# The last bit step of a weight conversion: low word rounded into the high word on ScalarE, high word masked in place on VectorE

## The chip, the core and the metric

One core of a Trainium2 chip runs the whole kernel. The metric is the device time of one execution in microseconds; 447.03 us is the median of three runs before the change. The engines are named as the profile names them: PE is TensorE (matmuls; PEld its weight loads), DVE is VectorE, ACT is ScalarE, POOL is GpSimd, SP is the engine that issues most DMAs.

## The reference

An mLSTM cell feeds a two-layer MLP with a quick gelu. Cut to what matters:

```python
# cell: B, H, S, D = 4, 8, 768, 40, step by step over t
C = f_stab * C + i_stab * outer(v_t, k_t);  n = f_stab * n + i_stab * k_t
y[t] = sigmoid(o_t) * (C @ q_t) / max(|n . q_t|, 1)
# bridge: (B, H, S, D) -> x of (3072, 320)
# MLP
'w_in':  np.random.randn(320, 2048).astype(np.float32) * (1.0 / np.sqrt(320))
'w_out': np.random.randn(2048, 320).astype(np.float32) * (1.0 / np.sqrt(2048))
h = x @ w_in
g = h * (1.0 / (1.0 + np.exp(-1.702 * h)))
out = g @ w_out
```

The factor behind `astype` is a 64-bit float, so both weight matrices arrive as 64-bit floats. The change concerns only how they become 32-bit floats.

## The kernel before

The sequence is cut into six windows of 128 steps. For each window the kernel does the cell as attention within the window plus a carried state, then the MLP for the window's 512 rows: up-projection, gelu, down-projection. The first window uses plain 32-bit matmuls (`up`, L657 and L666; `down`, L835). Later windows use other forms (L806, L888, L963) with weights that are split further on the core. The order on every engine is written out by hand: the program text is the order.

**The conversion.** The weights come in 20 pieces of 128 x 512 numbers, each fetched (L177, on SP's queue) as pairs of 32-bit words into a tile `bits`; `lo` is every even word and `hi` every odd one. Pieces 0, 1, 3, 4, 5, 6, 8 and 9 make w_in, pieces 2 and 7 make w_in_x (its last 64 rows), pieces 10 to 19 make w_out. The high word of a 64-bit float holds the sign, 11 bits of exponent and 20 of mantissa; a 32-bit float wants 8 bits of exponent and 23 of mantissa. Each piece passes through these steps:

- `convert_high` (L253, ScalarE): absolute value of the high word, read as a 32-bit float, into the destination.
- `convert_low` (L257, ScalarE): the low word times 2^-29, rounded to an integer from 0 to 8, in place. These are the three missing mantissa bits.
- `convert_clamp` (L269, VectorE): limits on the destination, so that the exponent fits.
- `convert_sign` (L274 and L276, VectorE): the destination is shifted left by 3 and its two top bits are cleared; then the two top bits of the high word (sign and top exponent bit) are put in with a two-operand operation.
- `convert_add` (L282, VectorE): the rounded low word is added as an integer. This add appears in the profile as a custom operation on 1024 16-bit elements.

The call order is: piece 0 among the attention of the first window, with high, clamp and sign before the low step; piece 1 in the seam behind it (high, then low, then the VectorE steps); pieces 1 to 5 finish in and after the seam into `up(0, 0)`; pieces 6 to 16 stand around the later pairs of up-projections; piece 17 stands before the first block of the down-projection (L1163 to L1168), pieces 18 and 19 before its fifth and sixth blocks. In between, VectorE does the gates, the transposes (L415) and the products with the weights (L493) for the attention of window 1, whose matmuls (L490, L534, L542) are laid between the blocks of the down-projection (L835).

On ScalarE the gelus (L672), copies (L409, L574) and exps (L452, L463) share the queue with the two conversion steps. GpSimd masks the attention weights (L454, L470) and scales values (L619).

Of the kernel before, what the change touches and what calls it, by code (L numbers as in the profile page):

```python
# [8 lines left out]
FP = mybir.dt.float32  # L9
FR = mybir.dt.float32r  # L10
U32 = mybir.dt.uint32
BF = mybir.dt.bfloat16
AF = mybir.ActivationFunctionType
OP = mybir.AluOpType
# [17 lines left out]
def kernel(  # L32
# [37 lines left out]
    op = ctx.enter_context(tc.tile_pool(name="op", bufs=2))  # L70
# [5 lines left out]
    V, A, G, T = nc.vector, nc.scalar, nc.gpsimd, nc.tensor  # L76
# [58 lines left out]

    w_in_bits, w_out_bits = moe_w_in.bitcast(U32), moe_w_out.bitcast(U32)
    rest_bits = w_in_bits[256:DM, :].rearrange("k (j two m) -> two k j m", two=2, m=256)
# [27 lines left out]
    bits = {}  # L165

    def fetch(n):
        if n < 3 or 10 <= n < 13:
            bits[n] = win.tile([128, 512, 2], U32, tag="wb", name="bits")
        elif n == 17:  # L170
            bits[n] = t_flat[:, at_bits:at_bits + 1024].bitcast(U32).rearrange("p (a two) -> p a two", two=2)
        else:
            bits[n] = (gp if 6 <= n < 10 else sp).tile([128, 512, 2], U32, tag="g", name="bits")
        for r, c, src in pieces[n][1]:
# [17 lines left out]

    small = t_flat[:, at_const:].bitcast(BF)
    idle, ident_b, neg_mask = (small[:, n * 128:n * 128 + 128] for n in range(3))
# [26 lines left out]
    for j in range(3):  # L221
        V.tensor_scalar(out=pick[j * BH:(j + 1) * BH, :], in0=ident[0:BH, 0:BH], scalar1=-1.0, scalar2=None,
                        op0=OP.mult)
# [16 lines left out]
    def words(n):  # L240
        return bits[n][:, :, 0], bits[n][:, :, 1], pieces[n][0]
# [5 lines left out]
    def convert_begin(n):  # L247
        convert_high(n)
        convert_low(n)
# [4 lines left out]

    def convert_low(n):
        lo, hi, dst = words(n)
        A.activation(out=lo, in_=lo, func=AF.Copy, scale=2.0 ** -29)  # L257

    def convert_end(n):
        convert_mid(n)  # L260
        convert_add(n)

    def convert_mid(n):
        convert_clamp(n)
        convert_sign(n)
# [5 lines left out]
    def convert_sign(n):  # L271
        lo, hi, dst = words(n)
        dst_u = dst.bitcast(U32)
        V.tensor_scalar(out=dst_u, in0=dst_u, scalar1=3, scalar2=0x3FFFFFFF, op0=OP.logical_shift_left,  # L274
                        op1=OP.bitwise_and)
        V.scalar_tensor_tensor(out=dst_u, in0=hi, scalar=0xC0000000, in1=dst_u, op0=OP.bitwise_and,  # L276
                               op1=OP.bitwise_or)

    def convert_add(n):
        lo, hi, dst = words(n)  # L280
        dst_u = dst.bitcast(U32)
        V.tensor_tensor(out=dst_u, in0=dst_u, in1=lo, op=OP.add)  # L282


    def split(engine, dst, x, left, part):

        first, second, third = (dst[j * BH:(j + 1) * BH, :] for j in range(3))
        engine.tensor_copy(out=first, in_=x)
        engine.tensor_tensor(out=left, in0=x, in1=first, op=OP.subtract)
        engine.tensor_copy(out=part, in_=left)  # L290
        A.copy(out=second, in_=part)
        engine.tensor_tensor(out=left, in0=left, in1=part, op=OP.subtract)
        engine.tensor_copy(out=third, in_=left)
# [5 lines left out]
    def gates(w):  # L299
# [8 lines left out]
        if w == 0:  # L308
            room = work.tile([L, H, D1], FP, tag="u", name="room").rearrange("p h d -> p (h d)")
            neg, part = room[0:BH, 0:L], room.bitcast(BF)[0:BH, 2 * L:3 * L]  # L310
            V.tensor_tensor(out=neg, in0=f_run, in1=i_sb[w], op=OP.subtract)
            split(G, a3, neg, neg, part)
        V.tensor_tensor_scan(out=m_run, data0=ones, data1=a, initial=m, op0=OP.mult, op1=OP.max)
        if w == 0:

            room = work.tile([L, H, D1], FP, tag="u", name="room").rearrange("p h d -> p (h d)")
            left, part = room[0:BH, 0:L], room.bitcast(BF)[0:BH, 2 * L:3 * L]
            split(V, m3, m_run, left, part)
# [669 lines left out]
    for b in range(B):  # L988
        if b >= 2:
            transposes(0, b)  # L990
            open_first(b - 2)
            weights(0, b)
            values(0, b - 2)
            scale(0, 0, b - 2, 2)
        else:
            weights(0, b)
        if b == 0:
            convert_high(0)
            transposes(0, 1)
        scores(0, b)  # L1000
        if b == 0:
            convert_mid(0)
        if b == 1:
            columns(0)
            convert_low(0)
            convert_add(0)
# [8 lines left out]
    seam(0, 0, 1)  # L1015
    seam(0, 1, 0)
    convert_low(1)

    def last_seam():
        seam(0, 1, 1)  # L1020
        convert_mid(1)
        convert_add(1)
        for p in (2, *converted[0][0]):
            convert(p)
# [217 lines left out]
```

## Time and profile before

| what | us |
|---|---|
| median of three runs (445.67 to 449.79) | 447.03 |
| the profiled execution | 443.5 |
| its span | 441.8 |
| TensorE busy, 4967 matmuls | 435.5 |
| VectorE busy, 701 instructions | 350.6 |
| ScalarE busy, 536 instructions | 245.6 |
| GpSimd busy, 133 instructions | 129.9 |

The prices of the conversion, from groups by line and shape (mean of one, ns): L253 681 to 684, L257 687, L269 418 to 525, L274 427 to 618, L276 692 to 731, L282 691 to 789, all on 128 x 512 numbers. The larger means contain instructions that ran beside GpSimd's work; the medians are 683, 687, 420, 427, 692 and 693.

How to read it: the span is the profiled stretch on the core, and the execution's own time is 1.7 us longer. In timelines the columns are start, duration, engine, line, operation, output and input tiles, shapes and count; what stands in brackets is idle time before and what ended it. In the chain of waits the columns are start, duration and what ran. A line number is that of the kernel before.

### The profile page before, as it was taken

What the parts mean: (1) busy time and instruction counts of PE and PEld (TensorE: products, weight loads), DVE (VectorE), ACT (ScalarE), POOL (GpSimd) and SP (SyncE); (2) the same over time, 40 slices, a digit from 0 to 9 for tenths busy, and PEclk for the clock granted to TensorE, in tenths of its full rate; (3) what the DMA queues carried; (4) which work ended last, traced back from release to release, by engine and by line L of the source; (5) the groups of instructions that cost most, each with busy time, mean ns of one, the idle gap of its engine ahead of it and who ended that gap; (6) DMA issues with size and microseconds to landing.
All of it is one profiled execution on the core that took longest, in us unless ns stands there. A gap on an engine that the chain in (4) does not pass through costs nothing.

```text
span 441.8 us, 12222 instructions
## 1 busy us (share of the span) xinstructions
PE 435.5 (99%) x4967; PEld 380.3 (86%) x4967; DVE 350.6 (79%) x701; ACT 245.6 (56%) x536; POOL 129.9 (29%) x133
## 2 busy tenths in 40 slices
PE   8999999999999999999999999999999999999996
PEld 6867887777889999888999888999888999888996
DVE  6888999989998877778686779686769666988990
ACT  5686779802987601677701586900486902397720
POOL 6401328530076600145600034700035610022100
PEclk9999999999999999999999999999999999999999
DMA  8999999228679238979026978306998306710000
GB/s 169 174 301 223 247 252 188 61 60 204 154 206 185 38 77 237 239 117 173 6 63 184 282 94 177 45 27 155 306 136 158 62 19 146 255 75 0 6 27 30
DMA packets 130008, 61.37 MB, mean 139 GB/s; under 512 B 102128, under 2 KB 122592, under 8 KB 129952
## 3 DMA queue, kind: packets, MB, share of 16 engines
q1 hardware_dynamic: 120512, 54.86, 56.6%
q10 hardware_dynamic: 8768, 4.28, 3.4%
q0 software_dynamic: 672, 1.46, 1.2%
q8 instruction: 39, 0.64, 0.6%
q14 instruction: 17, 0.14, 0.2%
HBM read 49.76 MB, written 10.81 MB: 137 GB/s over the span
## 4 chain that ended last, share of the span: by engine, by line
PE 79%; DMA 7%; DVE 6%; SPq 4%; ACT 2%; issue 1%; DVEq 0%
PE p_out L888 28%; PE p L806 17%; PE p_h L806 17%; PE p L963 6%; PE p_out L835 4%; SPq L132 3%; DMA bits<-in_moe_w_out_dram 3%; PE p L534 2%; PE p L542 2%; DMA q_sq<-in_q_dram 2%; PE p L490 2%; DMA bits<-in_moe_w_in_dram 1%; PE p L633 1%; DMA v_st<-in_v_dram 1%; DVE qT L415 1%
## 5 line engine op out<-in xcount | busy, mean ns | idle before, releaser
L856 POOL TENSOR_TENSOR g<-g 128x512 f32<-128x512 f32 x16 | 20.6, 1294 | 119.5 <-ACT g L784 119.5
L888 PE MATMUL p_out<-w_out,g 128*128 128x160 f32 x384 | 55.2, 300 | 0.0
L888 PEld LDWEIGHTS p_out<-w_out,g 128*128 128x128 f32 x384 | 53.1, 190 | 0.5
L765 ACT ACTIVATE x_high<-xT 128x512 fp32r<-128x512 f32 x10 | 6.3, 630 | 76.4 <-DVE xT L603 76.4
L784 ACT ACTIVATE g<-g 128x512 f32<-128x512 f32 x80 | 46.4, 628 | 2.6 <-DVE g L825 2.3
L823 ACT ACTIVATE g<-p 128x512 f32<-128x512 f32 x40 | 21.7, 596 | 36.4 <-PE p L806 35.0
L825 DVE SCALAR_TENSOR_TENSOR g<-p,g 128x512 f32<-128x512 f32 x40 | 25.7, 682 | 18.4 <-ACT g L823 10.1
L463 ACT ACTIVATE wt<-wt,cols 128x64 f32<-128x64 f32 x160 | 38.9, 335 | 0.1
L893 DVE TENSOR_TENSOR o_sb<-o_sb,p_out 128x160 f32<-128x160 f32 x56 | 16.7, 316 | 26.9 <-PE p_out L888 26.8
L888 PE MATMUL p_out<-t_sb,s 128*128 128x160 f32 x256 | 37.8, 301 | 0.0
L888 PEld LDWEIGHTS p_out<-t_sb,s 128*128 128x128 f32 x256 | 35.5, 190 | 0.2
L835 PE MATMUL p_out<-w_out,g 128*128 128x320 f32 x128 | 35.7, 436 | 0.0
L835 PEld LDWEIGHTS p_out<-w_out,g 128*128 128x128 f32 x128 | 23.9, 190 | 9.6
L825 DVE SCALAR_TENSOR_TENSOR g<-p_h,g 128x512 f32<-128x512 f32 x40 | 26.1, 683 | 5.8 <-PE p_h L806 5.0
L657 PE MATMUL p_h<-xT,w_in 128*128 128x256 f32 x128 | 29.8, 385 | 0.7 <-ACT xT L574 0.7
L657 PEld LDWEIGHTS p_h<-xT,w_in 128*128 128x128 f32 x128 | 23.6, 190 | 6.1 <-issue 2.2
L823 ACT ACTIVATE g<-p_h 128x512 f32<-128x512 f32 x40 | 23.3, 595 | 8.5 <-PE p_h L806 8.5
L470 POOL TENSOR_SCALAR_AFFINE_SELECT wt<-wt 64x1024 f32<-64x1024 f32 x20 | 24.6, 1231 | 6.9 <-ACT wt L463 5.8
L806 PE MATMUL p_h<-x_diff,w_diff 128*128 128x512 f32 x80 | 25.1, 394 | 0.0
L806 PE MATMUL p_h<-x_rest,w_rest 128*128 128x512 f32 x80 | 25.0, 394 | 0.0
L806 PE MATMUL p<-x_rest,w_rest 128*128 128x512 f32 x80 | 25.0, 394 | 0.0
L806 PE MATMUL p<-x_diff,w_diff 128*128 128x512 f32 x80 | 25.0, 393 | 0.0
(226 smaller groups left out, 1045.9 us busy)
## 6 DMA issues: line engine op xcount, KB each, us to landing
w_diff<-w_row SPq DMA_DIRECT2D x16, 512.0 KB, 5.8
wt<-m_row SPq DMA_DIRECT2D x20, 256.0 KB, 5.4
bits<-in_moe_w_in_dram SPq DMA_DIRECT2D x8, 512.0 KB, 7.6
out_dram<-o_sb SPq DMA_DIRECT2D x24, 160.0 KB, 3.1
q_sq<-in_q_dram SPq DMA_DIRECT2D x10, 320.0 KB, 9.1
eo<-in_o_gate_dram SPq DMA_DIRECT2D x5, 640.0 KB, 5.5
bits<-in_moe_w_out_dram SPq DMA_DIRECT2D x8, 320.0 KB, 5.8
q_sq<-x_row SPq DMA_DIRECT2D x10, 256.0 KB, 2.7
```

The costliest lines, as they stand in the source:

```text
L463: A.activation(out=x[:, h, :], in_=x[:, h, :], func=AF.Exp, scale=-1.0, bias=cols[w][:, c * PH + h:c * PH + h + 1])
L470: G.affine_select(out=r, in_=r, compare_op=OP.is_ge, fill=0.0, base=0, pattern=[[0, PH], [1, HL]], channel_multiplier=-1)
L657: T.matmul(ph[j][i][:, t], w_in[f // 4][:, c, f % 4 * 128:f % 4 * 128 + 128], x[:, c, t], start=(first and c == 0 and n == 0), stop=(not f ...
L784: A.activation(out=g, in_=g, func=AF.Gelu_apprx_sigmoid)
L806: T.matmul(dst[i], a(i), x, start=(first and m == which[0]), stop=(last and m == which[-1]))
L823: A.activation(out=g[:, i, :], in_=side[i], func=AF.Copy, scale=-BASE)
L825: V.scalar_tensor_tensor(out=g[:, i, :], in0=main[i], scalar=1.0 + 1.0 / BASE, in1=g[:, i, :], op0=OP.mult, op1=OP.add)
L835: T.matmul(po, gs[w, f // 2][:, f % 2, b * L:(b + 1) * L], w_out_sb[f // NH][:, f % NH, :], start=(f == 0), stop=(f == NF - 1))
L856: G.tensor_tensor(out=a10, in0=a00, in1=a10, op=OP.subtract)
L888: T.matmul(po, a(f), b[:, f, :], start=(f == 0), stop=(f == NH - 1))
L893: V.tensor_tensor(out=dst, in0=x, in1=po, op=OP.add)
L963: T.matmul(dst, g_part[n, b, f // 2][:, f % 2], wo[n, f][0][:, wo[n, f][1]], start=(f == order[0] and n < 2), stop=(f == order[-1] and n > 0))
```

## The change

The low step on ScalarE writes its rounded integer as 16 bits into the lower half of the high word, in place of the whole low word. VectorE, in place of the two-operand operation on the high word and the destination, masks the high word in place, keeping its two top bits and its four lowest. The add then brings in the masked high word: sign, top exponent bit and rounded low bits in one.

```diff
+U16 = mybir.dt.uint16
...
     def convert_low(n):
         lo, hi, dst = words(n)
-        A.activation(out=lo, in_=lo, func=AF.Copy, scale=2.0 ** -29)
+        half = bits[n].rearrange("p a two -> p (a two)").bitcast(U16).rearrange("p (a four) -> p a four", four=4)
+        A.activation(out=half[:, :, 2], in_=lo, func=AF.Copy, scale=2.0 ** -29)
...
         V.tensor_scalar(out=dst_u, in0=dst_u, scalar1=3, scalar2=0x3FFFFFFF, op0=OP.logical_shift_left,
                         op1=OP.bitwise_and)
-        V.scalar_tensor_tensor(out=dst_u, in0=hi, scalar=0xC0000000, in1=dst_u, op0=OP.bitwise_and,
-                               op1=OP.bitwise_or)
+        V.tensor_scalar(out=hi, in0=hi, scalar1=0xC000000F, scalar2=None, op0=OP.bitwise_and)
...
     def convert_add(n):
         lo, hi, dst = words(n)
         dst_u = dst.bitcast(U32)
-        V.tensor_tensor(out=dst_u, in0=dst_u, in1=lo, op=OP.add)
+        V.tensor_tensor(out=dst_u, in0=dst_u, in1=hi, op=OP.add)
```

The number of instructions and their order on every engine stay as they are. The waits differ: the low step waits for ScalarE's own high step (for piece 0, for VectorE's mask); the mask waits for the DMA and ScalarE's low step, and no longer for the shift; the add waits for VectorE alone (for piece 0, for ScalarE's low step).

## The prediction

> **What bounds the kernel now.** I read the page's slices first, then the timelines of TensorE and VectorE over the stretch in which weights are converted (8 to 88 us), then the chain of waits there, then single lines for prices. The slices show TensorE busy throughout at the full granted clock.
>
> ```profile
> PE   8999999999999999999999999999999999999996
> DVE  6888999989998877778686779686769666988990
> PEclk9999999999999999999999999999999999999999
> ```
>
> A busy TensorE is not yet a bound, since waiting matmuls can count as busy. So I looked at its pace in the timeline (columns: start, duration, line, tile, shapes, count):
>
> ```profile
> 23.91 1.13 PE L657 MATMUL p_h<-xT,w_in 128*128 128x256 f32 x4 [0.70 <-ACT xT L574]
> ...
> 34.22 3.72 PE L657 MATMUL p_h<-xT,w_in 128*128 128x256 f32 x16
> 37.87 1.99 PE L666 MATMUL p_h<-xT,w_in_x 64*128 64x512 f32 x8
> 39.79 3.72 PE L657 MATMUL p_h<-xT,w_in 128*128 128x256 f32 x16
> ...
> 82.91 4.57 PE L835 MATMUL p_out<-w_out,g 128*128 128x320 f32 x16
> 87.54 1.32 PE L534 MATMUL p<-v_st,wt 64*64 64x41 f32 x63
> ```
>
> The first row starts with the last wait that this view names for TensorE: 0.70 us at 23.91. Afterwards every group starts where the former ends and sixteen L657 rows take 3.72 us wherever they stand; a group held up by data would be longer than its twins. TensorE has 63.95 busy us in the 64 us from 24 to 88. From 107 us on the chain of waits is matmul after matmul to the end. So from 23.9 us on the time is TensorE's own work, and the converting engines matter only where they are late.
>
> How late they are now, VectorE's timeline, one piece and the junction at 86 us:
>
> ```profile
> 51.56 0.42 DVE L269 TENSOR_SCALAR w_out<-w_out 128x512 f32<-128x512 f32 x1
> 52.01 0.43 DVE L274 TENSOR_SCALAR w_out<-w_out 128x512 uint32<-128x512 uint32 x1
> 52.47 0.69 DVE L276 SCALAR_TENSOR_TENSOR w_out<-bits,w_out 128x512 uint32<-128x512 uint32 x1
> 53.30 0.69 DVE L282 CUSTOM_DVE_ANT_0 w_out<-bits,w_out 128x1024 uint16<-128x1024 uint16 x1
> 53.91 0.42 DVE L269 TENSOR_SCALAR w_out<-w_out 128x512 f32<-128x512 f32 x1
> ...
> 86.27 2.35 DVE L493 TENSOR_TENSOR wt<-p,wt 128x1024 f32<-128x1024 f32 x2
> ```
>
> A piece costs 53.91 - 51.56 = 2.35 us: starts 0.45, 0.46, 0.83 and 0.61 us apart. TensorE's deadlines, from the starts of the matmuls that read a piece: the first w_in_x piece is done at 29.44, read at 29.63 (0.2 us spare); piece 4 at 34.15, read in the second half of the group at 34.22, about 36.1 (1.9); piece 14 at 63.41, read in the second w_out block, after 66.3 (2.9). The junction: L493's first half ends at 86.27 + 1.23 = 87.50, and L534, which reads it, starts at 87.54; but TensorE's own L835 group before it ends at 82.91 + 4.57 = 87.48. VectorE and TensorE arrive there together. The chain of waits walks back through VectorE at this point:
>
> ```profile
> 84.83 0.70 DVE w_out L276
> ...
> 86.27 1.23 DVE wt L493
> 87.50 0.04 issue
> 87.54 1.32 PE p L534 x63
> ```
>
> This is the trap of the case: the chain names L276, the very operation that goes, yet without it TensorE would be ready only 0.06 us sooner.
>
> **Part 1, L276 becomes a one-operand mask (20 times).** The trace has no in-place operation on every second word, so bounds from rows: the nearest by kind is L274, a one-operand bit operation on 512 uint32 words, 427 ns; the other end is L276 itself, 692 ns, if the stride loses the faster rate; farther out is L415's transpose of 512 elements, 1,091 ns, the row in which VectorE writes with a stride (every fourth word). I take 427 ns: the stride costs nothing in the rows that have it, since L276 reads every second word in 692 ns, as the contiguous L775 does (692 ns, same kind and size). The add behind it waited for ScalarE and VectorE (0.83 us between starts for 0.69 us of work); now it waits for VectorE alone, which may save up to 0.83 - 0.69 - 0.03 = 0.11 us more (0.03 is the gap between clamp and shift, which has one wait). A piece gains 0.27 to 0.37 us, 20 pieces 5.3 to 7.4 us of VectorE. A mask of 692 ns gains 0 to 0.11 us, one of 1,091 ns loses 0.29 to 0.40 us per piece.
>
> What comes of it at the end: at the first w_in_x piece nothing, as L666 follows its predecessor directly; at the junction 0.06 us. What is late next there is TensorE itself. Cover: TensorE's back-to-back groups; without it the end would move by what the junction shows, below.
>
> [...]
>
> **Part 2, the low word (ScalarE, L257, 20 times).** Output becomes 16 bits wide at every eighth byte. L253 (strided read, dense write) takes 683 ns and L257 (strided both ways) 687 ns, so stride is free there; narrow writes appear only small and dense (L291, 32x128 bf16, 294 ns). Taken: 687 ns; bounds 0.6 us (a copy of that size, L672's 0.60) to twice 687 if narrow writes cost double. The new output overlaps what the high step reads, so the low step now waits for the high step before it on the same engine. Starts are 0.57 us apart now; a dependent start comes at 0.68 + 0.04 (L742 starts 0.04 us after L741 ends), so 0.15 us more per piece. Queued behind it on ScalarE are the gelus: three pieces stand before the first one (31.14), which moves by 0.45 us, and the groups at 59.87 to 63.30 by the same. The banks of the first gelu are needed at 34.22 and it ends at 32.23, 2 us spare; ScalarE then idles 3.11, 2.00 and 2.57 us ahead of later gelus and catches up. Cost at the end: 0. If narrow writes doubled, three pieces would cost 2.1 us plus 0.45 against those 2 us, so at most 0.6 us. Mask behind low: the mask starts 0.9 us after the high step ended, the low step ends 0.72 us after it, so it is on time.
>
> **Part 3, piece 0 turns round.** There the mask is issued before the low step, so ScalarE's low step (11.49) must wait for VectorE's mask, which starts at 11.58 and ends between 12.0 and 12.6 (L276 took 1.00 us there, beside GpSimd's L454). ScalarE stands 0.6 to 1.2 us; behind it queue both L409 copies, the tanh and the exps of batch 2. TensorE's L479 at 14.11 needs the copies, done at 13.35: 0.76 us spare, so it slips 0 to 0.5 us. At 16.32 ScalarE waited 1.63 us for L406 anyway, and at 22.82 it waited 0.99 us for the DMA of piece 1, behind which stands the L574 copy that TensorE awaits at 23.91. That DMA was issued at 17.11 behind queue SP's earlier ones, untouched by the change. Cost: 0, at most 0.3 us.
>
> DMAs: fetches that reuse a bits buffer still wait for the same add; some also for ScalarE, long done. No instruction changes place on any queue.
>
> **Sum.** -0.06 + 0 + 0 = about -0.1 us on the profiled execution: 443.5 us (span 441.8 and 1.7 around it) becomes 443.4. That execution lies 3.5 us under the median of the three runs; I carry the difference to the median: 447.03 - 0.1 = 446.9 us.
>
> **Rivals.**
> - *The conversions were the bound after all.* For it: the chain through L276 between 66 and 87 us, VectorE busy 58.13 of 64 us. Against: TensorE's even pace. If only the stretch behind the last idle counted (pieces 18 and 19 and part of 17), 1.1 us: 445.9; if all 7.4 us came out, 439.6. Chance 0.06, of which 0.04 beyond 1%.
> - *Slower: the strided write in place is slow.* Mask at L415's price, 0.29 to 0.40 us more per piece. VectorE last idled at 40.71 (0.74 us); after that pieces 8 to 19 run behind each other into L493, which has no spare. 12 x 0.29 to 0.40 = 3.5 to 4.8 us: 450.5 to 451.8. It decides as soon as the mask with its waits exceeds today's 0.83 us, and passes 1% at 4.5/12 = 0.37 us more, a mask of about 1.06 us. For it: L415. Against: L276's and L257's free strides. Chance 0.12, half of it beyond 1%.
> - *ScalarE's new waits reach TensorE* (parts 2 and 3): 0.3 + 0.6 us, 447.8. Against: idle times of 1 to 3 us behind each. Chance 0.04.
> - *The mask gains nothing* (692 ns): time as forecast, and inside its 0.78.
>
> **Numbers.** The forecast has 0.78. One percent is 4.5 us, about the 4.1 us spread of the three runs and what a measurement can tell from no change. Faster by more: 0.04 from the first rival and 0.01 of scatter, 0.05. Slower: 0.06 from the second and 0.03 of scatter and the unseen, 0.09. Same: 0.86. The forecast's own scatter is some 2.4 us either way (the runs lie 1.4 below to 2.8 above their median); the range goes to 444.5, and up to 449.8 towards the slower rival.
>
> **What would show it.** Right: masks of some 0.43 us; pieces some 2.0 us apart; VectorE with new idle time before L493; L534 still straight behind L835 near 87.5; L657 groups still 3.72 us. ScalarE's low step starting some 0.72 us behind the high one. Wrong: a mask over 0.8 us, a gap in TensorE before the L534 or L666 groups, or a first L657 moved from 23.9.

## The result, and the profile after

The change made the kernel slower by about half a percent. Over 21 runs of each kernel, taken beside each other, the median is 448.3 us after (446.27 to 451.83) against 445.7 us before (443.87 to 449.79); the ratio is 1.0054, with a 95% interval of 1.0033 to 1.0074, which is 1.5 to 3.3 us. The profiled execution of after took 448.44 us, with a span of 446.7; that of before had 443.5 and 441.8.

In the changed kernel almost every line number is one higher: L259 is the low step, L278 the mask, L283 the add, L464 the exps, L119 the copies into q_sq, L491 the score matmuls, L836 the down-projection. The slices and busy times of its page:

```profile
PE 438.5 (98%) x4967; PEld 382.2 (86%) x4967; DVE 342.2 (77%) x701; ACT 258.6 (58%) x536; POOL 129.4 (29%) x133
...
PE   8999999899999999999999999999999999999996
...
DVE  5886974969989777779686779686778656978990
...
PEclk9999999899999999999999999999999999999999
```

VectorE has lost 8.4 us of work (350.6 before), as the change means it to. ScalarE has gained 13 us (245.6 before). And TensorE's row and its clock's row both have an 8 in the eighth slice, 78 to 89 us, where they had a 9. The reason for ScalarE's 13 us stands in its costliest new group (operation, shapes and count, then busy us, mean ns of one, idle time before):

```profile
L259 ACT ACTIVATE bits<-bits 128x512 uint16<-128x512 uint32 x19 | 25.8, 1359 | 1.4 <-DVE bits L278 0.9
```

The low step takes 1,359 ns instead of 687. TensorE's timeline over the stretch shown of before:

```profile
25.20 1.13 PE L658 MATMUL p_h<-xT,w_in 128*128 128x256 f32 x4 [0.52 <-ACT xT L575]
...
65.46 8.78 PE L836 MATMUL p_out<-w_out,g 128*128 128x320 f32 x32
...
84.04 1.16 PE L491 MATMUL p<-qT,kT 40*64 40x64 f32 x64 [1.72 <-DVE state L643]
85.52 1.48 PE L491 MATMUL p<-qT,kT 40*64 40x64 f32 x64 [0.32 <-DVE state L643]
86.92 5.88 PE L836 MATMUL p_out<-w_out,g 128*128 128x320 f32 x16
92.73 1.14 PE L535 MATMUL p<-v_st,wt 64*64 64x41 f32 x64
```

Before, the score matmuls of both halves were one group:

```profile
80.89 2.10 PE L490 MATMUL p<-qT,kT 40*64 40x64 f32 x128
```

L535 starts 5.19 us later than L534 did before (87.54); some groups on, the first L807 matmul is 4.90 us later (111.88 against 106.98), and the difference in span is 4.9. These rows add up to it within 0.1 us:

- 1.29 us lie before 25.20, where the first row stood at 23.91. The whole up-projection keeps that shift and adds nothing: the first L836 group starts at 65.46 against 64.10.
- 1.72 + 0.32 = 2.04 us are a gap before the two halves of L491, which waits for VectorE's state. Before, L490 had no wait.
- 0.32 + 1.31 us are matmuls at a lower clock: the second half of L491 takes 1.48 instead of 1.16, the sixteen L836 rows 5.88 instead of 4.57. The granted clock is 0.89 from 80 to 88 us and 0.90 from 88 to 96.

Shorter stretches show that these two means hide a step (bounds, length, busy us and count of TensorE, its weight loads, VectorE, ScalarE and GpSimd, granted clock, DMA share, GB/s):

```profile
85.00:86.00 1.00, 0.69 (x48) 0.55 (x41) 0.97 (x3) 1.00 (x2) 0.30 (x1) 1.00 0.14 45
...
87.00:88.00 1.00, 1.00 (x2) 0.76 (x3) 0.97 (x3) 1.00 (x2) 0.00 (x0) 0.50 0.99 264
...
90.00:91.00 1.00, 1.00 (x5) 0.71 (x4) 1.00 (x2) 0.97 (x2) 1.00 (x1) 1.00 0.00 0
```

Read in stretches of 0.1 us, the clock is 0.50 for 3.41 us, from 86.2 to 89.6, and 1.00 on both sides. Half of 3.41 us is 1.7 us of matmul time, and the two rows lost 1.63.

The sum is 4.96. The first part isn't the change: the start of this row jumps between profiles, 23.79 and 23.93 in two kernels below that contain most of the change, 25.91 in one that keeps the old conversion, and up to 26.10 in others. Without it the profile shows 3.7 us lost, more than the 2.6 of the medians; the lower clock, as the runs below show, doesn't come in every execution.

Where the gap comes from, the chain of waits tells (start, duration, what ran):

```profile
72.70 1.54 ACT wt L464 x7
...
76.60 0.62 ACT q_sq L119
...
78.85 3.02 DVE qT L416 x3
...
84.96 0.51 DVE state L643
85.52 1.48 PE p L491 x64
```

Sixteen exps and two copies on ScalarE, then VectorE's transposes, then the state, then TensorE. Before, ScalarE had these rows:

```profile
58.90 1.08 ACT L672 ACTIVATE g<-p_h 128x512 f32<-128x512 f32 x2 [2.57 <-PE p_h L666]
...
68.50 3.93 ACT L463 ACTIVATE wt<-wt,cols 128x64 f32<-128x64 f32 x16
72.45 1.26 ACT L118 COPY q_sq<-q_sq 32x512 f32<-32x512 f32 x2
```

The exps and the copies are some 4.2 us later now. The gelu ahead of them is 1.37 us later itself, with the shift of the up-projection; the rest comes from ScalarE's queue behind it:

```profile
60.27 1.09 ACT L673 ACTIVATE g<-p_h 128x512 f32<-128x512 f32 x2 [1.13 <-PE p_h L667]
61.24 0.69 ACT L254 ACTIVATE w_out<-bits 128x512 f32<-128x512 f32 x1
61.96 1.35 ACT L259 ACTIVATE bits<-bits 128x512 uint16<-128x512 uint32 x1
63.05 0.70 ACT L254 ACTIVATE w_out<-bits 128x512 f32<-128x512 f32 x1
...
71.60 1.36 ACT L259 ACTIVATE t_sb<-t_sb 128x512 uint16<-128x512 uint32 x1
72.70 3.88 ACT L464 ACTIVATE wt<-wt,cols 128x64 f32<-128x64 f32 x16
```

The 1.13 us in brackets is ScalarE's last idle time before the exps. From this gelu's start to the exps it is 12.43 us now and was 9.60 (58.90 to 68.50): 2.83 us more, in which four low steps stand, those of pieces 14 to 17. From one high step to the next, 61.24 to 63.05, ScalarE needs 1.81 us; with starts 0.57 us apart it needed 1.14, so each piece costs 0.67 more, and four 2.7. TensorE lost 2.04. What was spare could be read before the change:

```profile
74.11 4.01 DVE L415 STREAM_TRANSPOSE qT<-q_sq 128x512 f32<-128x512 f32 x4
...
79.67 0.50 DVE L642 TENSOR_TENSOR state<-p,state 128x328 f32<-128x328 f32 x1
...
81.15 0.50 DVE L642 TENSOR_TENSOR state<-p,state 128x328 f32<-128x328 f32 x1
```

The copies were done at 72.45 + 1.26 = 73.71, and the transposes, behind VectorE's work on piece 17, started 0.40 us later. The first half's state was done at 79.67 + 0.50 = 80.17, and L490 started 0.72 us later. So 1.12 us were spare ahead of the first half, and 2.83 - 1.12 = 1.71 us is its gap. The second half had less: its state was done at 81.65, and its matmuls began at some 81.9, half way through L490. It waits another 0.32 us now.

### The profile page after: what moved, and what is told of

The parts are those of the page before. It is cut to its first block, busy times and chain, and to the rows that moved or that the text cites. A ratio compares the mean times of both kernels' runs of the same rounds, so it can differ in the third digit from the quotient of the medians.

```text
span 446.7 us, 12202 instructions
## 1 busy us (share of the span) xinstructions
PE 438.5 (98%) x4967; PEld 382.2 (86%) x4967; DVE 342.2 (77%) x701; ACT 258.6 (58%) x536; POOL 129.4 (29%) x133
## 4 chain that ended last, share of the span: by engine, by line
PE 88%; SPq 3%; ACT 3%; issue 2%; DMA 2%; DVE 1%; ACTq 0%
PE p_out L889 28%; PE p L807 16%; PE p_h L807 16%; PE p L964 6%; PE p_h L658 6%; PE p_out L836 5%; SPq L133 3%; PE p L535 2%; PE p L491 2%; PE p L543 2%; PE p L634 2%; PE p_h L667 2%; DMA bits<-in_moe_w_in_dram 2%; ACT wt L464 1%; DVE qT L416 1%
## 5 line engine op out<-in xcount | busy, mean ns | idle before, releaser
L464 ACT ACTIVATE wt<-wt,cols 128x64 f32<-128x64 f32 x160 | 38.8, 333 | 0.1
L836 PE MATMUL p_out<-w_out,g 128*128 128x320 f32 x128 | 37.0, 447 | 0.0
L836 PEld LDWEIGHTS p_out<-w_out,g 128*128 128x128 f32 x128 | 24.7, 196 | 10.1 <-issue 0.8
L259 ACT ACTIVATE bits<-bits 128x512 uint16<-128x512 uint32 x19 | 25.8, 1359 | 1.4 <-DVE bits L278 0.9
L807 PE MATMUL p_h<-x_diff,w_diff 128*128 128x512 f32 x80 | 25.1, 394 | 0.0
L807 PE MATMUL p<-x_rest,w_rest 128*128 128x512 f32 x80 | 25.0, 394 | 0.0
L807 PE MATMUL p_h<-x_rest,w_rest 128*128 128x512 f32 x80 | 25.0, 394 | 0.0
```

The source lines that it names most:

```text
L259: A.activation(out=half[:, :, 2], in_=lo, func=AF.Copy, scale=2.0 ** -29)
L464: A.activation(out=x[:, h, :], in_=x[:, h, :], func=AF.Exp, scale=-1.0, bias=cols[w][:, c * PH + h:c * PH + h + 1])
L807: T.matmul(dst[i], a(i), x, start=(first and m == which[0]), stop=(last and m == which[-1]))
L836: T.matmul(po, gs[w, f // 2][:, f % 2, b * L:(b + 1) * L], w_out_sb[f // NH][:, f % NH, :], start=(f == 0), stop=(f == NF - 1))
```

## The experiments

Three theories stood against each other. Of the width: the low step is slow for what it writes, and four such steps delay the exps, the copies, the state and TensorE. Of the waits: the new ones do it, low behind high and mask behind low. Of VectorE: the in-place mask or the add does it. The edits are against the changed kernel unless another is named, and each ratio is against the kernel before.

**Narrow write without the waits.** The 16-bit result goes to the low word's own low half, so that it doesn't touch what the high step and the mask use; the low word is not in the sum.

```diff
-        A.activation(out=half[:, :, 2], in_=lo, func=AF.Copy, scale=2.0 ** -29)
+        A.activation(out=half[:, :, 0], in_=lo, func=AF.Copy, scale=2.0 ** -29)
```

> The changed kernel, but the 16-bit result of the low step goes into the lower half of the low word, so it overlaps nothing that the high step reads, and neither ScalarE's low step nor VectorE's mask waits for it. The three rounded bits do not reach the result: the add brings in four mantissa bits of the high word instead. Width theory (a 16-bit output at every eighth byte doubles the low step): the low step still takes 1.36 us, ScalarE is still nearly full from 24 to 78 us, and TensorE still stands before L491; some 0.15 us less per piece, so 1.5 to 2.5 us above the kernel before. Dependence theory (the low step's wait for the high step is what costs): low step as before, time as before within 0.5 us. Start theory (the turn at piece 0 delays the first L657): time as before, first L657 back near 23.9.

The ratio is 1.0055 (1.0032 to 1.0078), as slow as the change. The low step has a mean of 1,367 ns, and in TensorE's timeline the gap is there:

```profile
84.32 1.16 PE L491 MATMUL p<-qT,kT 40*64 40x64 f32 x64 [1.17 <-DVE state L643]
```

With the 0.31 of the second half it is 1.48 us, 0.56 less than with the waits. From gelu to exps ScalarE needs 11.83 us (61.14 to 72.97), 2.23 more than before, and 2.23 less the 1.12 us that were spare is 1.11, close to the gap of 1.17.

**Wide write without the waits.** The low step as before the change; the mask and add of the change stay, so that here too the low word is not in the sum.

```diff
-        A.activation(out=half[:, :, 2], in_=lo, func=AF.Copy, scale=2.0 ** -29)
+        A.activation(out=lo, in_=lo, func=AF.Copy, scale=2.0 ** -29)
```

> The changed kernel with the low step of before: 32 bits, in place, on the low word. The mask and the add stay those of the change; the rounded bits do not reach the result, the add brings in four mantissa bits of the high word instead. This is VectorE's part of the change alone. Width theory and the prediction's cover: low step 0.69 us, VectorE's pieces some 1.9 us apart instead of 2.35, no gap in TensorE before L491, time as before within 0.5 us although VectorE has 7 us less to do. If VectorE's work had been the bound, up to 7 us faster.

The ratio is 0.9991 (0.9966 to 1.0016). The gap is gone:

```profile
81.85 2.10 PE L490 MATMUL p<-qT,kT 40*64 40x64 f32 x128
83.88 4.57 PE L835 MATMUL p_out<-w_out,g 128*128 128x320 f32 x16
```

This answers the theory of VectorE, and more: VectorE has 8.7 us less work here than before (341.9 against 350.6), with nothing to pay for it, and the time doesn't move. That is the forecast of Part 1 measured alone.

**Wide write with all the waits.** The low step writes 32 bits over the high word, so that it waits for the high step and the mask for it; signs are lost.

```diff
-        A.activation(out=half[:, :, 2], in_=lo, func=AF.Copy, scale=2.0 ** -29)
+        A.activation(out=hi, in_=lo, func=AF.Copy, scale=2.0 ** -29)
```

> The changed kernel, but the low step writes 32 bits over the whole high word, so it has every wait of the change (for the high step; at piece 0 for the mask) and a wide output. The sign and the upper exponent bits of the weights are left out of the result. Width theory: low step 0.69 us, 0.72 us behind the start of the high step, time as before within 0.7 us. Dependence theory: 2 to 3 us slower, as the change. Start theory: first L657 late by about 1 us, and the time with it.

The ratio is 0.9981 (0.9956 to 1.0006). ScalarE's rows show the wait: a low step starts 0.71 us behind its high step instead of 0.56 (59.75 and 60.46). For four pieces that is 0.6 us, less than the 1.12 spare ahead of the first half and just about what the second half had (L490 takes 2.21 us here instead of 2.10), so alone it costs nothing that the ratio shows. On top of doubled low steps, where the spare time is used up, it makes the gap 0.56 us longer. The theory of the waits falls as the cause and stays as a part.

**The prices by themselves.** Behind the end of the changed kernel, single operations on spare tiles: `mb` (pairs of words; `mb_lo` every even word, `mb_4` its 16-bit quarters) and `md` (uint16; `md_f` the same as bf16). VectorE's follow behind these:

```diff
+        A.activation(out=mb_lo, in_=mb_lo, func=AF.Copy, scale=2.0 ** -29)
+        A.activation(out=mb_4[:, :, 2], in_=mb_lo, func=AF.Copy, scale=2.0 ** -29)
+        A.activation(out=mb_4[:, 0:256, 2], in_=mb_lo[:, 0:256], func=AF.Copy, scale=2.0 ** -29)
+        A.activation(out=md[:, 0:512], in_=mb_lo, func=AF.Copy, scale=2.0 ** -29)
+        A.activation(out=md[:, 0:1024:2], in_=mb_lo, func=AF.Copy, scale=2.0 ** -29)
+        A.activation(out=md_f[:, 0:2048:4], in_=mb_lo, func=AF.Copy, scale=2.0 ** -29)
+        A.activation(out=md_f[:, 0:512], in_=mb_lo, func=AF.Copy, scale=2.0 ** -29)
...
```

> The changed kernel with two rounds of single ScalarE and VectorE operations behind its end, on tiles of their own, to be read as prices: 32 bits at every eighth byte; 16 bits at every eighth byte with 512 and 256 elements; 16 bits dense; 16 bits at every fourth byte; bf16 at every eighth byte; bf16 dense; on VectorE the mask, bf16 at every eighth byte and bf16 dense. Width theory in the form 'each strided narrow write costs a second step': 0.69 us wide, 1.36 strided narrow of either type, about 0.7 for 256 elements plus the fixed part, 0.69 dense. If the conversion to an unsigned 16-bit integer is what is slow: 1.36 for dense uint16 too, and 0.69 for bf16 at every eighth byte. A VectorE bf16 write at every eighth byte: 0.43 if only ScalarE pays, 0.8 or more if it is the memory that pays.

ScalarE's timeline: 32-bit output at every eighth byte (L1222), uint16 at every eighth byte (L1223), the same with 256 elements (L1224), uint16 dense (L1225), uint16 at every fourth byte (L1226), bf16 at every eighth byte (L1227) and dense (L1228):

```profile
445.11 0.66 ACT L1222 ACTIVATE mb<-mb 128x512 uint32<-128x512 uint32 x1
445.80 1.33 ACT L1223 ACTIVATE mb<-mb 128x512 uint16<-128x512 uint32 x1
447.17 0.77 ACT L1224 ACTIVATE mb<-mb 128x256 uint16<-128x256 uint32 x1
447.69 0.69 ACT L1225 ACTIVATE md<-mb 128x512 uint16<-128x512 uint32 x1
448.41 0.77 ACT L1226 ACTIVATE md<-mb 128x512 uint16<-128x512 uint32 x1
449.22 1.33 ACT L1227 ACTIVATE md<-mb 128x512 bf16<-128x512 uint32 x1
450.58 0.65 ACT L1228 ACTIVATE md<-mb 128x512 bf16<-128x512 uint32 x1
```

Neither the stride alone (0.66) nor the narrow type alone (0.69, 0.65) costs anything. The pair at every eighth byte costs double (1.33); at every fourth byte it costs only 0.08 us more than the dense one (0.77). From 256 to 512 elements it grows by 0.56 us, 2.2 ns for each element. The mask in place took 429 ns, and VectorE pays for the pair as well:

```profile
451.34 0.73 DVE L1230 TENSOR_SCALAR md<-mb 128x512 bf16<-128x512 f32 x1 [2.87 <-ACT md L1228]
452.11 0.43 DVE L1231 TENSOR_SCALAR md<-mb 128x512 bf16<-128x512 f32 x1
```

The first writes bf16 at every eighth byte, the second densely.

**Which pieces.** The change for pieces 14 to 17 alone, and in a second kernel for all but these:

```diff
+        if not (14 <= n <= 17):
+            A.activation(out=lo, in_=lo, func=AF.Copy, scale=2.0 ** -29)
+            return
```

with the old sign step and add under the same condition, which is reversed in the second kernel.

> The change for pieces 14 to 17 alone, the other sixteen converted as before. The width theory says where the loss arises: in the changed kernel ScalarE last stood idle, waiting for TensorE, just before the gelu at 60.27, so what the low steps cost before that is paid by then; between it and the exps of L464 lie the low steps of pieces 14 to 17, and the exps start 72.70 - 68.50 = 4.20 us later, 1.29 of which is the later start of the first L657. Expected: the exps about 2.8 us late, TensorE waiting 1.5 to 2 us before L491, and the whole loss of the change, 2 to 3 us. Rival (all twenty low steps add up): 4 of 20 of it, 0.5 us.

> The reverse: pieces 14 to 17 as before, the other sixteen as in the change, so that 16 of the 20 doubled low steps remain. Width theory with its place: ScalarE's excess before 60 us is taken up by its idle time before the gelus, TensorE does not wait before L491, time as before within 0.7 us. Rival (all twenty add up): 2 us slower.

Four pieces give the whole loss, 1.0078 (1.0044 to 1.0112); the other sixteen, piece 0 with its turned order among them, give 1.0001 (0.9973 to 1.0029). In the first kernel the score matmuls are L498 and the down-projection L843:

```profile
83.66 1.16 PE L498 MATMUL p<-qT,kT 40*64 40x64 f32 x64 [1.73 <-DVE state L650]
85.14 1.16 PE L498 MATMUL p<-qT,kT 40*64 40x64 f32 x64 [0.31 <-DVE state L650]
86.23 4.57 PE L843 MATMUL p_out<-w_out,g 128*128 128x320 f32 x16
```

The gap is the same 2.04 us. But here the clock stayed at 1.00, and the sixteen rows took their 4.57. So the lower clock isn't a fixed part of the gap. Every run lists its mean granted clock. Over some 446 us one stretch of 3.41 us at half clock makes a mean of 0.996, and two make 0.992, which allows a split: of this kernel's ten runs, five had at least 0.998 and a median of 447.58, and five had 0.991 or 0.992 and a median of 449.97. Against 445.33, the median of the runs of before that had at least 0.998, the first five lost 2.25 us, about the gap. Split the same way, the kernel with the narrow write and no waits lost 446.58 - 445.28 = 1.30 us for a gap of 1.48, in five of its eleven runs. So few runs give these sizes only roughly.

**A gap of another cause.** To the kernel before, masks that change nothing are added on VectorE just ahead of the transposes, two in one kernel and five in another:

```diff
                 convert_end(17)
+                dst_u = words(17)[2].bitcast(U32)
+                for _ in range(2):
+                    V.tensor_scalar(out=dst_u, in0=dst_u, scalar1=0xFFFFFFFF, scalar2=None, op0=OP.bitwise_and)
```

> The same with two such operations, some 0.9 us on VectorE. If the gap costs its own length: 0.5 to 0.9 us. If a short gap too lowers the granted clock: 1.8 us or more, with a sixteen-row L835 group above 5 us; if only a longer gap does: the group stays at 4.57 us.

> The kernel before, with five VectorE operations of 0.43 us behind piece 17 that leave their data as it is, so that L415 and all behind it on VectorE come 2 us or more later and TensorE stands for some 2 us before L490, with nothing of the change in it. To see what such a gap costs. If only its own length: 2 us. If the lower granted clock seen behind the gap of the changed kernel (0.89 and 0.90 in the stretches from 80 to 96 us) belongs to the gap: 2 us, and 1.3 to 1.6 us more in the L490 and L835 rows behind it, sixteen L835 rows taking 5.5 to 5.9 us instead of 4.57.

The sizes were missed: beside GpSimd's work two of these operations took 4.29 us and five took 7.68, and not 0.43 each. The gaps before L490 were thus 2.90 and 6.30 us, and the ratios 1.0119 (1.0082 to 1.0155) and 1.0203 (1.0158 to 1.0248), so 5.3 and 9.0 us. The kernel with two:

```profile
85.24 3.69 PE L490 MATMUL p<-qT,kT 40*64 40x64 f32 x128 [2.90 <-DVE state L642]
88.86 6.17 PE L835 MATMUL p_out<-w_out,g 128*128 128x320 f32 x16
```

and its stretches (columns as in the stretches of the changed kernel):

```profile
80.00:88.00 8.00, 5.11 (x113) 4.09 (x115) 7.79 (x13) 7.53 (x9) 2.92 (x3) 0.83 0.30 82
88.00:96.00 8.00, 8.00 (x124) 5.67 (x116) 5.30 (x8) 0.00 (x0) 4.41 (x3) 0.74 0.01 2
```

After the gap L490 takes 3.69 instead of 2.10 and L835 6.17 instead of 4.57, together 3.2 us more, as in the kernel with five (3.69 and 6.51, 3.5 us more). The two stretches give, as an estimate, some 6.9 us at a clock of 0.50 (8 us with a mean of 0.83 and 8 with 0.74, and 1.00 on both sides). In the kernel with five the clock is 0.50 over the whole stretch from 88 to 96, with 0.91 in the 8 us before it and 0.95 in the 8 us behind it, by the same estimate some 10.2 us; there the fall begins inside the gap. With no change in the conversion at all, a late VectorE at this place gives the same picture as the change did, gap and clock. None of these twelve runs kept a clock of 0.998.

**Moving the copies ahead.** If only the exps in front of the copies are in the way, the copies can go first. In the changed kernel, and as a control in the kernel before:

```diff
-                weights_exp(1, 0)
                 fill_squares(q_sq)
+                weights_exp(1, 0)
```

> The changed kernel with one exchange in ScalarE's order: the two copies that complete q_sq for VectorE's L416 (L119) stand ahead of the sixteen exps of L464 instead of behind them. If the loss runs from the doubled low steps over the late exps to these copies, and from them over L416 and L643 to TensorE's L491, the copies come some 3.9 us earlier, TensorE does not wait before L491, and the time is that of the kernel before within 0.7 us, with all twenty low steps still at 1.36 us. If the loss comes from somewhere else, or the exps themselves (1.3 us later, over GpSimd's mask) are what TensorE waits for, it stays 2 to 3 us slower.

> The same exchange in the kernel before, as a control: TensorE waits for nothing there now, so the time stays within 0.5 us. Any gain here would have to be taken off what the exchange repairs in the changed kernel.

This failed as a repair: 1.0057 (1.0033 to 1.0081) with the change, and the control itself is slower than the kernel before, 1.0038 (1.0013 to 1.0063). The aimed-at gap did go (changed kernel):

```profile
83.08 1.16 PE L491 MATMUL p<-qT,kT 40*64 40x64 f32 x64
85.51 1.16 PE L491 MATMUL p<-qT,kT 40*64 40x64 f32 x64 [1.27 <-DVE state L643]
```

The first half waits no longer, but the second now waits 1.27 us. The exps are later, hence GpSimd's work on them too, and one of its operations now runs beside VectorE's state product L611, which takes 2.17 us instead of 0.50:

```profile
81.53 3.04 POOL L848 TENSOR_TENSOR t_sb<-w_out 128x1280 f32<-128x1280 f32 x1
...
82.76 2.17 DVE L611 TENSOR_TENSOR state<-state_mid,cols 128x328 f32<-128x328 f32 x1
```

In the control L610 meets the same operation (2.16 us), and TensorE waits 0.32 us before the second half and 1.41 before L534. So it is shown that the first wait came through the copies; the exchange only trades it for another. With 0.44 us before L535 the waits shown are 1.7 us of the 2.5 that the changed kernel still loses with the exchange (447.85 against 445.36); where the rest goes is not shown.

## Why the prediction was wrong, point by point

The forecast was 0.1 us faster; the kernel became 2.6 us slower.

**TensorE bounds the kernel: right.** With 8.7 us less work on VectorE and the low step of before the ratio is 0.9991. That waiting can count as busy shows in the kernel with the wide write and all the waits: L490 took 2.21 us instead of 2.10, and TensorE counts 8.00 busy us in the 8 from 80 to 88.

**Part 1, mask 427 ns, a piece 0.27 to 0.37 us shorter, worth nothing: right, and a little low.** The mask's median is 428 ns, and a piece takes 54.44 - 52.58 = 1.86 us instead of 2.35 in VectorE's timeline:

```profile
52.58 0.42 DVE L271 TENSOR_SCALAR w_out<-w_out 128x512 f32<-128x512 f32 x1
...
53.38 0.42 DVE L278 TENSOR_SCALAR bits<-bits 128x512 uint32<-128x512 uint32 x1
53.84 0.69 DVE L283 CUSTOM_DVE_ANT_0 w_out<-bits,w_out 128x1024 uint16<-128x1024 uint16 x1
54.44 0.42 DVE L271 TENSOR_SCALAR w_out<-w_out 128x512 f32<-128x512 f32 x1
```

The gain is 0.49, the operation's 0.26 and the rest between starts. The rival of a slow strided write falls: the mask, in place on every second word, takes 428 ns and not the 1,091 of L415.

**Part 2, the low step: here the prediction failed, in two places.** The first is "Taken: 687 ns", argued from "stride is free there; narrow writes appear only small and dense". Each half is true by the rows above (0.66 and 0.69 us), but their sum doesn't follow: together they take 1,359 ns. The bound of "twice 687" held the value almost exactly.

The second is what that bound was said to cost, "at most 0.6 us". It was worked out for the three pieces in front of the first gelu alone, and the rest was left to the idle times of "3.11, 2.00 and 2.57 us ahead of later gelus". The last of these lies before the gelu at 58.90. Pieces 14 to 16, which the text names as "the groups at 59.87 to 63.30", and piece 17 come after it, with no idle time between them and the copies that the state waits for. Followed there, the bound would have given four times 0.69 + 0.15, some 3.4 us, for a state that had 0.40 + 0.72 us to spare in front of the first half of L490 and less in front of the second: a gap of 2.2 us or a little more. The measured gap was 2.04. That this estimate and the loss of 2.6 us come so close is partly luck: ScalarE needed 2.83 us more and not 3.4, and the loss also holds the lower clock of some executions.

The new wait of 0.15 us per piece was right (61.24 to 61.96 is 0.72). That it costs nothing held with low steps of the old length only. The rival "ScalarE's new waits reach TensorE" had the engine right, but the place and the price wrong.

**Part 3, piece 0: right.** ScalarE stood 0.87 us, within 0.6 to 1.2, and L480 waited 0.53 us, at the upper end of "0 to 0.5"; the kernel in which sixteen pieces, 0 among them, are changed has 1.0001.

**The signs.** "A gap in TensorE" was named as what would refute the forecast, but before L534 and L666; it came before L490, two groups ahead of L534, for which no deadline had been worked out. The lower clock behind it wasn't foreseen. The first L657 did move, with the landing of a DMA (24.10 against 22.82) and not with the change.

**What stays open.** In the sixteen of 21 runs of the change that kept a clock of 0.998 or more, the median is 448.26, 2.6 us over that of before, while the profiled gap is 2.04; the difference is within the interval. Why the pair of narrow and strided is slow was not tried, only its price.

## What to carry to other kernels

A store that is both narrower than a word and strided can have a price of its own, here twice that of 32-bit words at every eighth byte (1.33 against 0.66 us for 512 elements): neither the row of a strided wide store nor that of a dense narrow one (0.69) gives it, so time it alone or keep the upper bound in the sum. When an operation on a side engine may get longer, follow its queue from the engine's last idle time on to the next result that the bound engine waits for, not only to its first reader, and add up all the instances in between against that one deadline. A gap on the bound engine may cost more than its length: here the profiled execution lost another 1.6 us behind a gap of 2 us, so a deadline with 1 us to spare isn't comfortable.

## What the hardware showed unexpectedly

**Narrow strided writes.** ScalarE takes 2.2 ns for each 16-bit element at every eighth byte, and 1.33 us for 512, against 0.66 for 32-bit elements at the same step; at every fourth byte it is 0.77. VectorE takes 0.73 for bf16 at every eighth byte against 0.43 for dense. Dense 32-bit rows of before come to 0.84 ns for each element (128x1024 in L717 take 1.06 us and 128x512 in L765 0.63); the strided narrow ones to 2.2.

**The clock after a gap.** The granted clock fell to 0.50 for 3.41 us behind a gap of 2.04 us. Worked out from the means of the 8 us stretches, as above, it was there for some 3.4 us behind one of 1.48 (0.88 and 0.91), for some 6.9 behind one of 2.90 and for some 10.2 in and behind one of 6.30: close to once, twice and three times the same length. Whether it falls, the gap's own length doesn't fix: another gap of 2.04 us and one of 1.27 left it at 1.00. What decides it wasn't tried.

**VectorE beside GpSimd.** Two masks of 0.43 us took 4.29 us together in the kernel with two, beside GpSimd's L470 and L847 (2.96 us), and a two-operand product of 0.50 took 2.17, beside L848 (3.04 us).
